# Attention scores of the last two batches as three fp32r products, in a kernel of attention, dense MoE and routed experts

## The chip, the cores and the metric

The kernel runs on one core of one Trainium2 chip. The metric is the device time of one execution in microseconds (us). The core's engines are TensorE (PE, with its weight loads as PEld), VectorE (DVE), ScalarE (ACT), GpSimd (POOL) and SyncE (SP); SP issues nearly all the DMAs.

## The reference

Three stages, each fed by the one before. Inputs are fp32; batch 4, 12 heads, 448 positions, head size 64; the dense stage has 768 columns and 2048 hidden units; the routed stage has 8 experts of 1024.

```python
scores = scale * np.matmul(q, k.transpose(0, 1, 3, 2))
scores = cap * np.tanh(scores / cap)
scores = scores - np.max(scores, axis=-1, keepdims=True)
attn = np.exp(scores)
attn = attn / (np.sum(attn, axis=-1, keepdims=True) + 1e-09)
x = np.matmul(attn, v)
...
h = x @ w_in
g = np.maximum(h, 0.0) ** 2
x = g @ w_out
...
out[mask] = np.maximum(x[mask] @ w1[e], 0.0) @ w2[e]
```

The last line is done for each expert `e`, where `mask` holds the tokens that a greedy routing by the sorted gate logits gives it.

## The kernel before

**Attention** (`attention(b)`, L207) takes a batch in six head pairs `hp`. One tile `qk` (128 x 960) holds a pair: head 0 on partitions 0 to 63, head 1 on 64 to 127; columns 0 to 511 are k in four chunks `c`, the rest is q. `scores(hp, c)` (L225) multiplies in fp32. Chunks 0 to 2 are two matmuls, one for each head on its half of the rows (L234); chunk 3 holds what is left of both heads and is one matmul over all rows (L236). Each fp32 matmul leaves two MATMUL records in the trace. ACT then does tanh (L238) and exp (L239). The sums over the chunks, `z`, are added on POOL from batch 1 on (L245, L247, L251). `pv` (L253) multiplies by v, `norm` (L264) sums z over the partitions on PE (L267), adds an epsilon on ACT (L269), and DVE takes the reciprocal (L270) and multiplies (L272). In the last two batches (`whole`) the pieces of a pair come in larger steps.

**Dense stage.** `hidden(b)` (L387) makes 16 tiles of 18 matmuls of the type fp32r, `output(b)` (L422) six tiles of 48. Every operand is split into a high and a low fp32r part (a cast on ACT, a subtraction on DVE or POOL), and a product is the sum of three, high by high, low by high and high by low (L400 to L402, L457 to L459). The attention's result is split so by `split_rows` (L310). The weights come as 64-bit words: DVE rebuilds fp32 from them in three instructions a tile (L329 to L331), ACT casts the high part (`wh`, L357), POOL or DVE subtracts (`wl`, L358), and both are stored to DRAM (L376), from where the later batches load them. That is done once, beside the first two batches: the 16 tiles of w_in, then the 24 of w_out.

**Order.** `run` (L87) does attention(0), then hidden(0) beside attention(1), then for b = 2 and 3 output(b-2) and hidden(b-1) beside attention(b). `merge` (L906) takes the next piece from the stream that is least far along: each piece yields a number of us, and a stream has a total (118.0 and 44.0). From b = 2 on this written order is PE's own. All the other engines, and SP's DMAs, are put in order by the tile framework's scheduler. Every engine works through its instructions in that order, so an instruction that waits holds up what stands behind it on its engine.

**Names used below.** qk(b, hp) is a pair's tile; it has two buffers (L213), the load is on SP (L219). `load_v` (L221) has three. `g` is the dense stage's hidden tile (cast L411, subtraction L412), `r` its relu and square (L407, L408), `acc` the psum tile it comes from (two buffers), `raw` a tile of 64-bit words (three buffers), `wf` the rebuilt fp32 tile (three). `finish` (L432) transposes an output tile (L435), copies it (L437) into a tile `rows` of two buffers and stores it on ACT's queue (L438). `xt` (pool "rows", seven buffers) holds the tiles before that.

Of the kernel before, what the change touches and what calls it, by code (L numbers as in the profile page):

```python
# [9 lines left out]
F32 = mybir.dt.float32  # L10
F32R = mybir.dt.float32r
# [8 lines left out]
NB, NH, S, DH = 4, 12, 448, 64  # L20
# [3 lines left out]
HP = NH // 2  # L24
KC = 4
KP = S // KC
WAIT = (), (8, 12, 16)
KB = S // 128
# [52 lines left out]
class Kernel:  # L81
# [5 lines left out]
    def run(self):  # L87
        tc = self.tc
        PS = bass.MemoryType.PSUM
        with tc.tile_pool(name="keep", bufs=1) as self.keep, \  # L90
                tc.tile_pool(name="wts", bufs=1) as self.wts, \
                tc.tile_pool(name="psum", bufs=2, space=PS) as self.psum, \
                tc.tile_pool(name="dram", bufs=1, space=bass.MemoryType.DRAM) as self.dram, \
                ExitStack() as right, ExitStack() as left:
            self.setup()
            self.mp = right.enter_context(tc.tile_pool(name="moe1", bufs=1, side="right"))
            self.gpool = self.mp
            xs = right.enter_context(ExitStack())
            self.xp = xs.enter_context(tc.tile_pool(name="x", bufs=ND, side="right"))
            with tc.tile_pool(name="x32", bufs=ND, side="right") as self.xq:  # L100
                with tc.tile_pool(name="rows", bufs=ND + 1, side="right") as self.tp, \
                        tc.tile_pool(name="attn", bufs=2, side="right") as self.ap:
                    merge([(self.attention(0), 44.0)])
                    self.split_rows(0)
                    merge([(self.hidden(0), 58.0), (self.attention(1), 44.0)])
                    for b in range(2, NB):
                        self.split_rows(b - 1)
                        streams = [(chain(self.output(b - 2), self.hidden(b - 1)), 118.0), (self.attention(b), 44.0)]
                        if b == NB - 1:
                            streams.append((self.gate_decode(), 30.0))  # L110
                        with tc.manual_schedule(engines={mybir.EngineType.PE}):
                            merge(streams)
                self.split_rows(NB - 1)
            self.gp = left.enter_context(tc.tile_pool(name="gate", bufs=1))
            last = left.enter_context(ExitStack())
            self.gpool = last.enter_context(tc.tile_pool(name="last", bufs=1))
            with tc.tile_pool(name="gate_load", bufs=3, side="right") as self.gl:
                with tc.manual_schedule(engines={mybir.EngineType.PE}):
                    merge([(self.hidden(NB - 1), 60.0), (self.gate_weights(), 80.0)])
            xs.close()  # L120
            self.tp = right.enter_context(tc.tile_pool(name="rows2", bufs=2, side="right"))
            self.rp = right.enter_context(tc.tile_pool(name="route", bufs=1, side="right"))
            self.router_setup()

            def room():
                last.close()
                self.ep = left.enter_context(tc.tile_pool(name="expert", bufs=2))

            with tc.manual_schedule(engines={mybir.EngineType.PE}):
                self.second(room)  # L130
# [76 lines left out]
    def attention(self, b):  # L207

        nc, ap = self.nc, self.ap
        qk, P, vt, zs, U = {}, {}, {}, {}, {}  # L210
        adder = nc.vector if b == 0 else nc.gpsimd

        def load(hp):  # L213
            qk[hp] = t = ap.tile([128, QK], F32, name="qk", bufs=2)
            if b + hp == 0:
                for half, q in ((0, nc.sync), (1, nc.scalar)):
                    q.dma_start(t[half * 64:half * 64 + 64], self.q_k[b, hp, half * 64:half * 64 + 64])
            else:
                nc.sync.dma_start(t, self.q_k[b, hp])  # L219

        def load_v(hp):  # L221
            vt[hp] = ap.tile([128, KB + 1, 2 * DH], F32, name="v", bufs=3)
            nc.sync.dma_start(vt[hp], self.v[b, hp])

        def scores(hp, c):  # L225

            t = qk[hp]
            n = 2 if c < KB else 1
            k, q = t[:, c * 128:(c + 1) * 128], t[:, QK - S:]
            ps = self.psum.tile([128, 2, 512], F32, name="big")  # L230
            if c < KB:
                for s in range(2):
                    rows = slice(s * 64, s * 64 + 64)
                    nc.tensor.matmul(ps[:, s, :S], k[rows], q[rows], start=True, stop=True)  # L234
            else:
                nc.tensor.matmul(ps[:, 0, :S], k, q, start=True, stop=True)  # L236
            p = ap.tile([128, n, S], F32, name=f"p{n}", bufs=(2, 5)[n - 1])
            nc.scalar.activation(p, ps[:, :n, :S], AF.Tanh, scale=self.isc)  # L238
            e = nc.scalar.activation(p, p, AF.Exp, scale=self.capt)  # L239
            if b == 0:  # L240
                self.exps.append(e)
            P[hp, c] = p
            if c == 1:
                zs[hp] = z = ap.tile([128, 2, S], F32, name="z", bufs=2)
                adder.tensor_add(z, P[hp, 0], p)  # L245
            elif c == 2:
                adder.tensor_add(zs[hp], zs[hp], p)  # L247
            elif c == KB:
                for s in range(2):
                    half = slice(s * 64, s * 64 + 64)  # L250
                    adder.tensor_add(zs[hp][half, s], zs[hp][half, s], p[half, 0])  # L251

        def pv(hp, c0, c1):  # L253
            if c0 == 0:
                U[hp] = self.psum.tile([128, S], F32, name="aux")
            for c in range(c0, c1):
                if c < KB:
                    for s in range(2):
                        nc.tensor.matmul(U[hp][s * 64:s * 64 + 64], vt[hp][:, c, s * 64:s * 64 + 64], P[hp, c][:, s],  # L259
                                         start=(c == 0), stop=False, skip_group_check=True)  # L260
                else:
                    nc.tensor.matmul(U[hp], vt[hp][:, c], P[hp, c][:, 0], start=False, stop=True, skip_group_check=True)

        def norm(hp):  # L264
            z = self.psum.tile([128, S], F32, name="aux")
            for s in range(2):
                nc.tensor.matmul(z[s * 64:s * 64 + 64], self.ones, zs[hp][:, s], start=True, stop=True)  # L267
            d = zs[hp][:, 0]
            (nc.vector.tensor_scalar(d, z, self.eps, None, op0=OP.add) if b == 0 else nc.scalar.activation(d, z, AF.Identity, bias=self.eps))  # L269
            nc.vector.reciprocal(d, d)  # L270
            x = self.xq.tile([128, S], F32, name="x")
            m = nc.vector.tensor_mul(x, U.pop(hp), d)  # L272
            if b == 0:
                self.norms.append(m)
            if b == NB - 1:
                self.mark = m
            self.x_t[b, hp] = x

        load(0)
        load(1)  # L280
        load_v(0)
        whole = b > 1
        for hp in range(HP + 1):
            if hp < HP:
                if hp + 1 < HP:
                    load_v(hp + 1)
                scores(hp, 0)
                if not whole:
                    yield 0.8
                scores(hp, 1)  # L290
                yield 1.6 if whole else 0.8
            if hp:
                pv(hp - 1, 0, 2)
                if not whole:
                    yield 1.6
                pv(hp - 1, 2, 4)
                if not whole or hp == HP:
                    yield 1.6
                norm(hp - 1)
                yield 4.0 if whole else 0.8  # L300
            if hp < HP:
                scores(hp, 2)
                if not whole:
                    yield 0.8
                scores(hp, 3)
                if hp + 2 < HP:
                    load(hp + 2)
                yield 1.4 if whole else 0.6

    def split_rows(self, b):  # L310
        nc = self.nc
# [110 lines left out]
    def output(self, b):  # L422
# [9 lines left out]
        def finish(j, xt):  # L432
            ps = self.psum.tile([KP, KC, 128], F32, name="aux")
            for c in range(KC):
                nc.tensor.transpose(ps[:, c], xt[:, c * KP:(c + 1) * KP], self.c("ident"))  # L435
            o = mp.tile([KP, KC, 128], F32, name="rows", bufs=2)
            (nc.vector.tensor_copy if b == LAST and j == ND - 1 else nc.scalar.copy)(o, ps)  # L437
            nc.scalar.dma_start(  # L438
                rows[j // DA][b, :, :, j % DA * 128:(j % DA + 1) * 128], o)
# [520 lines left out]
```

## Time and profile before

| | |
|---|---|
| runs | 1087.70, 1090.86, 1092.13 us, median 1090.86 |
| profiled execution | 1092.94 us, of which the span is 1091.2 |
| mean granted clock of PE | 0.99 |
| busy PE, DVE, ACT, POOL | 1058.7 (97%), 597.1 (55%), 469.1 (43%), 247.8 (23%) us |
| matmuls of the scores (L234, L236) | 74.7 us and about 2% of the span on the chain that ended last |

The page gives busy time over the whole span. A stage in which a second engine is as full as PE doesn't show there; for that, busy time by stretch is needed. In the timelines a start is in us from the span's start, and a bracket at the end of a row tells how long the engine was idle before it and which instruction ended that. PE's rows overlap, because a matmul's record is longer than the distance to the next one.

### The profile page before, as it was taken

The page shows a single profiled execution, that of the slowest core. Times are in us where ns is not written, and L with a number is a line of the kernel's source. Part 1 is how long each engine was busy: PE and PEld are TensorE (multiplying, and loading weights), DVE is VectorE, ACT ScalarE, POOL GpSimd, SP SyncE. Part 2 cuts the span into 40 slices and gives each one's busy share as a digit, 9 for nine tenths or more (in the row PEclk, how much of TensorE's full clock was granted, in tenths as well). Part 3 has the DMA queues.
Part 4 walks back from the last instruction along what each step waited for, and adds up shares of the span by engine and source line. Part 5 has one row for each costly group of instructions (what it writes and reads, how often), then busy time and mean ns, then how long its engine had stood idle before and what let it go on. Part 6 is the DMA issues. An engine that isn't in the chain of part 4 may idle for free.

```text
span 1091.2 us, 15936 instructions
## 1 busy us (share of the span) xinstructions
PE 1058.7 (97%) x5866; PEld 836.0 (77%) x5866; DVE 597.1 (55%) x1068; ACT 469.1 (43%) x723; POOL 247.8 (23%) x181
## 2 busy tenths in 40 slices
PE   6899999999999999999999999998899999999996
PEld 2336656777678677677888888887799999999996
DVE  5997999997222245465311253445445444676550
ACT  5867686445554533454543000012232222544551
POOL 0217684764221322221000000002220201012000
PEclk9999999999999999999999999998999999999998
DMA  8644777899655499987984467567466257656620
GB/s 280 239 142 149 252 261 259 256 329 322 209 181 174 153 305 331 340 293 267 311 298 134 153 185 249 187 179 225 133 241 233 71 183 246 216 184 218 216 81 26
DMA packets 102494, 237.54 MB, mean 218 GB/s; under 512 B 11088, under 2 KB 21872, under 8 KB 102416
## 3 DMA queue, kind: packets, MB, share of 16 engines
q1 hardware_dynamic: 87776, 219.58, 59.8%
q0 software_dynamic: 3424, 11.19, 3.4%
q10 hardware_dynamic: 11216, 5.75, 2.0%
q8 instruction: 46, 0.75, 0.3%
q14 instruction: 32, 0.26, 0.1%
HBM read 194.01 MB, written 42.47 MB: 217 GB/s over the span
## 4 chain that ended last, share of the span: by engine, by line
PE 76%; issue 11%; DVE 7%; DMA 3%; ACT 2%; POOL 1%; SPq 0%; POOLq 0%; DVEq 0%; ACTq 0%
PE big L885 8%; PE acc L457 8%; PE acc L459 7%; PE acc L458 7%; PE acc L400 7%; PE acc L401 6%; PE acc L402 6%; PE acc L847 5%; PE big L234 4%; PE aux L259 4%; PE aux L661 2%; PE acc L854 2%; PE aux L267 2%; PE big L236 2%; DVE wf L330 1%
## 5 line engine op out<-in xcount | busy, mean ns | idle before, releaser
L457 PE MATMUL acc<-g,wh 128*128 128x448 f32 x384 | 151.5, 394 | 0.0
L400 PE MATMUL acc<-xh,wh 128*128 128x448 f32 x384 | 147.8, 387 | 0.8 <-ACT r L407 0.8
L401 PE MATMUL acc<-xl,wh 128*128 128x448 f32 x384 | 141.0, 367 | 0.8 <-DVE xl L317 0.8
L459 PE MATMUL acc<-g,wl 128*128 128x448 f32 x384 | 140.7, 366 | 0.0
L458 PE MATMUL acc<-g,wh 128*128 128x448 f32 x384 | 140.7, 366 | 0.0
L402 PE MATMUL acc<-xh,wl 128*128 128x448 f32 x384 | 140.1, 365 | 0.0
L885 PE MATMUL big<-wh,g 128*112 128x384 f32 x512 | 118.2, 343 | 0.0
L238 ACT ACTIVATE p<-big,isc 128x896 f32<-128x896 f32 x96 | 85.8, 908 | 44.8 <-PE big L234 36.9
L270 DVE RECIPROCAL z<-z 128x448 f32<-128x448 f32 x24 | 70.7, 2948 | 59.8 <-ACT z L269 59.7
L412 DVE TENSOR_TENSOR g<-r,g 128x448 fp32r<-128x448 f32 x58 | 42.9, 740 | 103.6 <-ACT g L411 103.3
L400 PEld LDWEIGHTS acc<-xh,wh 128*128 128x128 f32 x384 | 71.7, 187 | 33.9 <-issue 14.7
L764 POOL DMA_INDIRECT xg<-x,idx x32 | 34.5, 1078 | 257.0 <-issue 157.7
L239 ACT ACTIVATE p<-p,capt 128x896 f32<-128x896 f32 x96 | 89.4, 948 | 1.5
L885 PEld LDWEIGHTS big<-wh,g 128*112 128x112 f32 x512 | 86.4, 175 | 0.8
L457 PEld LDWEIGHTS acc<-g,wh 128*128 128x128 f32 x384 | 73.0, 190 | 14.4 <-issue 9.6
L401 PEld LDWEIGHTS acc<-xl,wh 128*128 128x128 f32 x384 | 72.4, 189 | 11.4 <-issue 3.4
L234 PE MATMUL big<-qk 64*128 64x448 f32 x288 | 74.7, 602 | 6.5 <-DMA qk<-qk 6.3
L329 DVE TENSOR_SCALAR wf<-raw 128x512 int32<-128x512 int32 (+1 forms) x64 | 52.7, 837 | 46.5 <-DMA raw<-w_out_t 38.1
L407 ACT ACTIVATE r<-acc 128x448 f32<-128x448 f32 x64 | 34.7, 542 | 100.9 <-PE acc L402 87.6
L459 PEld LDWEIGHTS acc<-g,wl 128*128 128x128 f32 x384 | 72.5, 189 | 6.8 <-issue 0.2
L402 PEld LDWEIGHTS acc<-xh,wl 128*128 128x128 f32 x384 | 72.3, 188 | 6.9 <-issue 0.8
L458 PEld LDWEIGHTS acc<-g,wh 128*128 128x128 f32 x384 | 72.9, 190 | 6.0 <-issue 1.7
(181 smaller groups left out, 1865.2 us busy)
## 6 DMA issues: line engine op xcount, KB each, us to landing
g<-w SPq DMA_DIRECT2D x62, 384.0 KB, 6.9
wh<-wih SPq DMA_DIRECT2D x48, 384.0 KB, 3.5
wl<-wil SPq DMA_DIRECT2D x48, 384.0 KB, 5.6
wh<-woh SPq DMA_DIRECT2D x72, 256.0 KB, 3.0
wl<-wol SPq DMA_DIRECT2D x72, 256.0 KB, 2.9
wf<-w SPq DMA_DIRECT2D x33, 384.0 KB, 3.5
raw<-w SPq DMA_DIRECT2D x33, 384.0 KB, 4.4
raw<-w_in SPq DMA_DIRECT2D x16, 768.0 KB, 6.5
```

The costliest lines, as they stand in the source:

```text
L234: nc.tensor.matmul(ps[:, s, :S], k[rows], q[rows], start=True, stop=True)
L238: nc.scalar.activation(p, ps[:, :n, :S], AF.Tanh, scale=self.isc)
L239: e = nc.scalar.activation(p, p, AF.Exp, scale=self.capt)
L270: nc.vector.reciprocal(d, d)
L400: nc.tensor.matmul(ps, wh[:, d], xh, start=(d == 0), stop=False)
L401: nc.tensor.matmul(ps, wh[:, d], xl, start=False, stop=False)
L402: nc.tensor.matmul(ps, wl[:, d], xh, start=False, stop=(d == ND - 1))
L457: nc.tensor.matmul(ps, a, gh, start=(f == 0), stop=False)
L458: nc.tensor.matmul(ps, a, gl, start=False, stop=False)
L459: nc.tensor.matmul(ps, z, gh, start=False, stop=(f == NF - 1))
L847: nc.tensor.matmul(H[j], W[j][0][:, d], xs[:, d, 0].bitcast(F32), start=(d == 0), stop=(d == ND - 1))
L885: nc.tensor.matmul(acc[h][:, s, :DM // 2], l, r[:, s * (DM // 2):(s + 1) * (DM // 2)], start=(j == 0 and first), stop=(j == NF2 - 1 and last))
```

## The change

For batches 2 and 3 a new `split(hp)` makes a high and a low fp32r tile of the pair's `qk`, the cast on ACT and the subtraction on DVE. `scores` then does three fp32r products in place of one fp32 product, on the row halves as before. split(0) comes ahead of the batch's first pair, split(hp+1) behind scores(hp, 3). Each of the two new tiles has one buffer. `load_v(hp+1)` is moved behind norm(hp-1), for all batches; v has two buffers in place of three, `xt` six in place of seven, the output tile `rows` one in place of two. The attention's total is 47 in place of 44, and two of its yields change, which moves its pieces against the dense stage's on PE.

```diff
-                with tc.tile_pool(name="rows", bufs=ND + 1, side="right") as self.tp, \
+                with tc.tile_pool(name="rows", bufs=ND, side="right") as self.tp, \
...
-                        streams = [(chain(self.output(b - 2), self.hidden(b - 1)), 118.0), (self.attention(b), 44.0)]
+                        streams = [(chain(self.output(b - 2), self.hidden(b - 1)), 118.0), (self.attention(b), 47.0)]
...
+        whole = b > 1
...
         def load_v(hp):
-            vt[hp] = ap.tile([128, KB + 1, 2 * DH], F32, name="v", bufs=3)
+            vt[hp] = ap.tile([128, KB + 1, 2 * DH], F32, name="v", bufs=2)
             nc.sync.dma_start(vt[hp], self.v[b, hp])
 
+        def split(hp):
+            h, l = (ap.tile([128, QK], F32R, name=f"qk{i}", bufs=1) for i in "hl")
+            nc.scalar.copy(h, qk[hp])
+            nc.vector.tensor_sub(l, qk[hp], h.bitcast(F32))
+            qk[hp] = (h, h), (h, l), (l, h)
+
         def scores(hp, c):
 
-            t = qk[hp]
             n = 2 if c < KB else 1
-            k, q = t[:, c * 128:(c + 1) * 128], t[:, QK - S:]
+            products = qk[hp] if whole else ((qk[hp], qk[hp]),)
             ps = self.psum.tile([128, 2, 512], F32, name="big")
-            if c < KB:
-                for s in range(2):
-                    rows = slice(s * 64, s * 64 + 64)
-                    nc.tensor.matmul(ps[:, s, :S], k[rows], q[rows], start=True, stop=True)
-            else:
-                nc.tensor.matmul(ps[:, 0, :S], k, q, start=True, stop=True)
+            for i, (x, y) in enumerate(products):
+                k, q = x[:, c * 128:(c + 1) * 128], y[:, QK - S:]
+                first, last = i == 0, i == len(products) - 1
+                if c < KB:
+                    for s in range(2):
+                        rows = slice(s * 64, s * 64 + 64)
+                        nc.tensor.matmul(ps[:, s, :S], k[rows], q[rows], start=first, stop=last)
+                else:
+                    nc.tensor.matmul(ps[:, 0, :S], k, q, start=first, stop=last)
...
-        whole = b > 1
+        if whole:
+            split(0)
+            yield 3.0
         for hp in range(HP + 1):
             if hp < HP:
-                if hp + 1 < HP:
-                    load_v(hp + 1)
                 scores(hp, 0)
...
                 norm(hp - 1)
-                yield 4.0 if whole else 0.8
+            if hp + 1 < HP:
+                load_v(hp + 1)
+            if hp:
+                yield 3.2 if whole else 0.8
             if hp < HP:
                 scores(hp, 2)
...
                 scores(hp, 3)
                 if hp + 2 < HP:
                     load(hp + 2)
-                yield 1.4 if whole else 0.6
+                if whole and hp + 1 < HP:
+                    split(hp + 1)
+                yield 2.2 if whole else 0.6
...
-            o = mp.tile([KP, KC, 128], F32, name="rows", bufs=2)
+            o = mp.tile([KP, KC, 128], F32, name="rows", bufs=1)
```

In the rows of the order that follow, a name's number tells one buffer's use from another, and the bracket lists the engines and DMA queues that an instruction waits for. The line numbers of the changed kernel are 9 to 14 higher from `scores` on.

The first place is ACT's order at the end of attention(1). Here p2_1150 is a score tile of attention(1)'s last pair, acc_1137 a psum tile of hidden(0), and qk_1385 the tile qk(2, 0). Before:

```order
L238 ACTIVATE p1_1118<-big_1116,isc_70 128x448 [waits PE_49]
L408 ACTIVATE r_1110<-r_1110 128x448 [waits Activation_49]
L239 ACTIVATE p1_1118<-p1_1118,capt_66 128x448 [waits Activation_49]
L411 CAST g_1113<-r_1110 128x448 [waits Activation_49]
L238 ACTIVATE p2_1150<-big_1147,isc_70 128x896 [waits PE_49]
L357 CAST wh_1236<-wf_1181 128x512 [waits DMAHW3_49,DVE_49,PE_49]
L407 ACTIVATE r_1170<-acc_1137 128x448 [waits DVE_49,PE_49]
```

After:

```order
L248 ACTIVATE p1_1118<-p1_1118,capt_66 128x448 [waits Activation_49]
L425 CAST g_1113<-r_1110 128x448 [waits Activation_49]
L228 CAST qkh_1391<-qk_1385 128x960 [waits DMAHW5_49]
L247 ACTIVATE p2_1150<-big_1147,isc_70 128x896 [waits PE_49]
L371 CAST wh_1236<-wf_1181 128x512 [waits DMAHW2_49,DVE_49,PE_49]
L421 ACTIVATE r_1170<-acc_1137 128x448 [waits DVE_49,PE_49]
```

The cast of qk(2, 0), which waits for that tile's load, now stands between the cast of g_1113 and the tanh, the cast of wh_1236 and the relu.

The second place is SP's order at the same time: the loads of w_out and of qk, and the stores of the split weights (wih, wil, woh, wol). Before:

```order
L376 DMA wil14_1241<-wl_1130 128x768 [waits DMAHW4_49,Pool_49]
L325 DMA raw_1414<-w_out 128x512 [waits DMAHW5_49,DVE_49]
L219 DMA qk_1385<-qk 128x960 [waits DMAHW6_49,PE_49]
L376 DMA wih15_1298<-wh_1187 128x768 [waits DMAHW7_49,Activation_49]
L376 DMA wil15_1299<-wl_1188 128x768 [waits DMAHW0_49,Pool_49]
L325 DMA raw_1456<-w_out 128x512 [waits DMAHW1_49,DVE_49]
```

After:

```order
L390 DMA wil14_1241<-wl_1130 128x768 [waits DMAHW3_49,Pool_49]
L339 DMA raw_1402<-w_out 128x512 [waits DMAHW4_49,DVE_49]
L220 DMA qk_1385<-qk 128x960 [waits DMAHW5_49,PE_49]
L390 DMA wih15_1298<-wh_1187 128x768 [waits DMAHW6_49,Activation_49]
L390 DMA wil15_1299<-wl_1188 128x768 [waits DMAHW7_49,Pool_49]
L220 DMA qk_1387<-qk 128x960 [waits DMAHW5_49,DMAHW0_49,DVE_49]
L390 DMA woh0_1375<-wh_1236 128x512 [waits DMAHW1_49,Activation_49]
L339 DMA raw_1428<-w_out 128x512 [waits DMAHW2_49,DVE_49]
```

The load of qk(2, 0) stands where it stood, behind a load of w_out that waits for DVE. The next qk tile is now loaded ahead of the w_out tile that used to come, and it waits for DVE (for the subtraction of the first pair, whose tile it overwrites).

The third place is DVE's order between the decode of the twelfth tile of w_out (wf_1656 before, wf_1669 after) and what follows it in attention(2). Before:

```order
L331 SCALAR_TENSOR_TENSOR wf_1627<-raw_1628,wf_1627 128x512 [waits DVE_49]
L329 TENSOR_SCALAR wf_1656<-raw_1657 128x512 [waits DMAHW0_49,DVE_49]
L330 SCALAR_TENSOR_TENSOR wf_1656<-raw_1657,wf_1656 128x512 [waits DVE_49]
L331 SCALAR_TENSOR_TENSOR wf_1656<-raw_1657,wf_1656 128x512 [waits DVE_49]
L270 RECIPROCAL z_1405<-z_1405 128x448 [waits Activation_49]
```

After:

```order
L345 SCALAR_TENSOR_TENSOR wf_1640<-raw_1641,wf_1640 128x512 [waits DVE_49]
L343 TENSOR_SCALAR wf_1669<-raw_1670 128x512 [waits DMAHW0_49,DVE_49]
L344 SCALAR_TENSOR_TENSOR wf_1669<-raw_1670,wf_1669 128x512 [waits DVE_49]
L345 SCALAR_TENSOR_TENSOR wf_1669<-raw_1670,wf_1669 128x512 [waits DVE_49]
L229 TENSOR_TENSOR qkl_1575<-qk_1387,qkh_1574 128x960 [waits PE_49,Activation_49]
L343 TENSOR_SCALAR wf_1712<-raw_1713 128x512 [waits DMAHW1_49,Pool_49]
```

The subtraction for pair 1 of attention(2) stands behind that tile's decode. On PE the pair's first scores, which read qkl_1575, stand about where pv(0) of attention(2) stood before.

## Rows read from the trace of the kernel before

**Rows 1.** Busy time by stretch: us, PE, PEld, DVE, ACT, POOL, clock, DMA, GB/s.

```profile
140.00:170.00 30.00, 30.00 (x129) 18.08 (x126) 29.66 (x19) 22.77 (x35) 26.85 (x15) 1.00 0.73 247
...
200.00:230.00 30.00, 30.00 (x144) 22.07 (x144) 29.54 (x27) 14.37 (x23) 21.26 (x13) 1.00 0.88 288
```

**Rows 2.** PE's timeline around a pair's scores in attention(2): start, us, engine, line.

```profile
301.61 0.37 PE L400 MATMUL acc<-xh,wh 128*128 128x448 f32 x1
...
302.01 0.37 PE L402 MATMUL acc<-xh,wl 128*128 128x448 f32 x1
302.31 1.77 PE L234 MATMUL big<-qk 64*128 64x448 f32 x8
...
304.33 0.36 PE L401 MATMUL acc<-xl,wh 128*128 128x448 f32 x1
```

**Rows 3.** The same timeline, cut at 302.80.

```profile
302.31 1.02 PE L234 MATMUL big<-qk 64*128 64x448 f32 x4
```

**Rows 4.** Timeline of PE's weight loads.

```profile
301.61 0.19 PEld L401 LDWEIGHTS acc<-xl,wh 128*128 128x128 f32 x1
```

**Rows 5.** Groups by form: line, engine, operation, count | busy us, mean ns | idle before.

```profile
L357 ACT CAST wh<-wf 128x768 fp32r<-128x768 f32 x40 | 33.1, 831 | 33.3 <-DMA wf<-w 13.1 <-PE acc L854 9.9 <-PE big L885 6.7
...
L358 DVE TENSOR_TENSOR wl<-g,wh 128x768 fp32r<-128x768 f32 x48 | 45.9, 955 | 22.3 <-ACT wh L357 19.9 <-issue 1.1 <-PE acc L854 0.9
```

**Rows 6.** ACT's timeline at the end of attention(1).

```profile
155.77 0.56 ACT L411 CAST g<-r 128x448 fp32r<-128x448 f32 x1
157.63 1.01 ACT L238 ACTIVATE p<-big,isc 128x896 f32<-128x896 f32 x1 [1.30 <-PE big L234]
...
159.04 0.55 ACT L407 ACTIVATE r<-acc 128x448 f32<-128x448 f32 x1
```

**Rows 7.** SP's timeline: the load of qk(2, 0).

```profile
163.49 0.69 SPq L219 DMA_DIRECT2D qk<-qk  x1
```

**Rows 8.** The loads of L219 in 150 to 180: issue to landing in us.

```profile
DMA to landing us min/median/max: 7.3/7.3/7.3
```

**Rows 9.** PE's timeline: a tile of hidden(0), norm(1, 5), pv(2, 0).

```profile
168.59 0.47 PE L400 MATMUL acc<-xh,wh 128*128 128x448 f32 x1
...
182.90 0.97 PE L267 MATMUL aux<-z,ones 128*64 128x448 f32 x2
...
203.48 1.35 PE L259 MATMUL aux<-p,v 128*64 128x448 f32 x6
```

**Rows 10.** DVE's timeline.

```profile
161.38 1.65 DVE L331 SCALAR_TENSOR_TENSOR wf<-raw,wf 128x512 int32<-128x512 int32 x1
...
166.54 0.61 DVE L412 TENSOR_TENSOR g<-r,g 128x448 fp32r<-128x448 f32 x1
167.07 2.33 DVE L329 TENSOR_SCALAR wf<-raw 128x512 int32<-128x512 int32 x1
...
171.75 0.42 DVE L329 TENSOR_SCALAR wf<-raw 128x512 int32<-128x512 int32 x1
...
178.18 0.61 DVE L272 TENSOR_TENSOR x<-aux,z 128x448 f32<-128x448 f32 x1
...
212.57 0.69 DVE L331 SCALAR_TENSOR_TENSOR wf<-raw,wf 128x512 int32<-128x512 int32 x1
```

**Rows 11.** POOL's timeline: what runs beside the third of those rows.

```profile
166.76 2.35 POOL L245 TENSOR_TENSOR z<-p,p 128x896 f32<-128x896 f32 x1 [2.72 <-DVE x L272]
```

**Rows 12.** ACT's timeline: two copies of output tiles in a row.

```profile
255.26 0.57 ACT L437 COPY rows<-aux 112x512 f32<-112x512 f32 x1
...
266.78 0.59 ACT L437 COPY rows<-aux 112x512 f32<-112x512 f32 x1 [2.45 <-PE aux L435]
```

**Rows 13.** Issue to landing of those stores.

```profile
DMA to landing us min/median/max: 3.3/4.8/8.4
```

**Rows 14.** PE's timeline in attention(0): an idle stretch.

```profile
20.47 1.66 PE L267 MATMUL aux<-z,ones 128*64 128x448 f32 x3 [3.10 <-DVE z L251]
```

**Rows 15.** Busy time by stretch, behind it; columns as in Rows 1.

```profile
20.60:24.00 3.40, 3.40 (x8) 0.85 (x7) 2.51 (x4) 0.00 (x0) 0.00 (x0) 0.51 0.88 293
```

## The prediction

> **What bounds the kernel now.** I first read the busy time by stretch, because a mean over the span hides where a second engine is full. In 140 to 170 and in 200 to 230 PE is busy for the whole 30 us, at a granted clock of 1.00, and so is DVE, for 29.66 and 29.54 us [rows 1]. That is the stage in which the weights are rebuilt on DVE. The reader is to see two things: there a us more or less on PE is a us of the whole, and work that is put on DVE there has no free place. Next come PE's timeline, for the price of a score, and the timelines of ACT, SP and DVE at the places of the order shown above, for what the new instructions wait for.
>
> **PE: the gain.** A normal fp32r matmul starts every 0.20 us (two steps from 301.61 to 302.01) [rows 2]. Chunks 0 and 1 of a pair stand between the L402 at 302.01 and the L401 at 304.33; less the 0.20 of that L402 and of the L400 between them, they hold PE for 1.92 us. Their four fp32 products are eight records, two passes each [rows 2]. By 302.80 four of these have begun [rows 3]; one after the other at 0.20 us, the fourth would begin only at 302.91. So the two heads' halves run side by side, in four slots of about 0.37 us (four fill the 1.77 with a tail), and the remaining 0.4 us is the change to half rows and back. Chunks 2 and 3 are again four slots of two passes (one product on halves, one on all rows), so I count a pair as 2 x 1.92 = 3.84 us. After, chunks 0 and 1 are six slots of halves, chunks 2 and 3 three and three: twelve slots of 0.203, with the same 0.4 twice 3.27 us. The gain is 0.57 us a pair, 6.8 us for twelve pairs. Since PE is full there, all of it counts, if PE is not made to wait.
>
> The slots' price rests on fp32r loads of weights staying hidden: the load for L401 starts at 301.61 with the L400 of the same rows [rows 4], and the matmuls keep their 0.20.
>
> **ACT and DVE: the added work.** The cast of 128 x 960 is 960/768 of one of 0.831 us, 1.04 us; the subtraction is 960/768 of 0.955, 1.19 us [rows 5]; twelve of each. As busy time on ACT this is free, PE doesn't wait for ACT's throughput. On DVE, in the full stretch, it is not. Beside POOL a DVE row can be several times as long: the same L329 takes 2.33 us while POOL adds z from 166.76 on [rows 11], and 0.42 at 171.75 [rows 10]. So 1.19 is the lower end, some 2.5 the upper.
>
> **First wait: ACT behind a load.** The cast of qk(2, 0) stands in ACT's order ahead of the tanh of p2_1150. Before, ACT was through with the g cast at 156.33, the tanh began at 157.63 and the relu at 159.04 [rows 6]. But qk(2, 0) left SP only at 163.49 [rows 7], behind a load of w_out that waits for the decode which ends at 163.03 [rows 10], and took 7.3 us to land [rows 8], till about 170.5 counted from the issue's start, perhaps a us sooner. The order on SP is the same after. So ACT stands from 156.3 to about 170. Then come the cast 1.0 and what was 157.63 to 159.59 from tanh to the relu's end, 2.0: the relu is done at 172.6. The hidden(0) tile at 168.59 [rows 9] needs the psum buffer that this relu frees, so PE waits 4.0 us (bounds 2, if the load comes earlier, and 5). DVE's subtraction of g, 166.54 [rows 10], waits for ACT's cast of the same g, behind exp, square and cast (2 us more), till 174.6: 8 us in which DVE, which has no slack, stands still.
>
> Directly behind this is norm(1, 5) at 182.90 [rows 9]: its psum buffer is free when DVE has done the multiplication of 178.18 [rows 10]. With DVE 8 us behind and PE 6, 0 to 5 us are lost; I take 1, since most of the 8 is covered by PE's own lag and the 4 us between the two.
>
> **Second wait: qkl of pair 1 on DVE.** In DVE's new order this subtraction comes behind the twelfth decode of w_out, before done at 212.57 + 0.69 = 213.3 [rows 10]. PE comes to the pair's first scores about where pv(2, 0) was, 203.48 [rows 9]; with the first wait, its clock (below) and the 1 us, 210.2. The subtraction ends at 213.3 + 1.2 (that of pair 0) + 1.2 = 215.7 if DVE has made up its 8 us, because POOL too has less to do meanwhile, and at 223.7 if it hasn't: PE waits 5.5 or 13.5 us. A DVE which runs in its short forms throughout could take all of it away, so the lower bound is 0. I take 8, near the lower of the two, because the long forms leave DVE room to catch up. This wait doesn't depend on the first: without it DVE is 8 us earlier, but so is PE by 6.7. Pairs 2 and 3 stand behind further decodes: 0 to 3 us, I take 1. From 264 on no decode of these weights is left, and in attention(3) the cast and the subtraction have room.
>
> **The clock.** After 3.10 us without work [rows 14] PE ran 3.40 us at 0.51, its 1.2 GHz level [rows 15], which costs 1.7 us. Two long waits: 3.4 us; bounds 0 and 3.4.
>
> **Edits at nothing.** The output tile with one buffer: copies are at least 11.5 us apart [rows 12], a store lands 8.4 us after its issue at most [rows 13]; without this cover the transposes would wait for up to some 3 us each. v with two buffers, loaded behind the norm: a 256 KB load in the place of another, needed a whole pair later. The xt tiles: six are written a batch, and read long before the next batch's.
>
> **The sum.** -6.8 + 4.0 + 1.7 + 1 + 8 + 1.7 + 1 = +10.6 us, on the profiled execution's 1092.9 a time of 1103.5. The median is 2.1 below that execution, so 1101.5, **1102 us**. With the bounds (waits of 2, 0, 5.5, 0 and one drop of the clock, or 5, 5, 13.5, 3 and two) this case reaches from 1093 to 1114.
>
> **The rivals.** What a measurement of this kernel can tell from no change is about 0.5%, 5.5 us: 1085.4 and 1096.3.
>
> *DVE catches up, ACT's wait stays.* The qkl of pair 1 is ready at 210. For it: half of DVE's rows there are long forms. Against: 29.54 of 30 us busy [rows 1], and two subtractions more. -6.8 + 4.0 + 1.7 + 1 is 0: 1091.
>
> *Faster: both waits are covered.* The place is ACT's cast of qk(2, 0): if its load lands by 157.6 no wait starts, and DVE loses no time. The load would have to leave SP some 13 us sooner than at 163.49, or the scheduler's place for the cast be harmless; and qkl of pair 1 would have to be done by 203.5, 10 us ahead of its decode's end before. Then the gain of 6.8 stands alone: 1084. It decides when all waits and clock drops are together under 1.3 us.
>
> *The halves don't run side by side in fp32r.* Nine slots of a pair are doubled, 9 x 0.203 x 12 = 22 us: 1124. Against: fp32 halves do [rows 3], and nothing in the edit changes the rows they use.
>
> *Weight loads come into the open.* In the twelve slots of a pair two or three products follow each other on the same rows. If a load had to wait for the matmul ahead of it, each slot would be 0.19 us longer [rows 4], 144 x 0.19 = 27 us: 1129. Against: the normal matmuls alternate weights on the same rows at 0.20. The Trainium skill ("TensorE: Matmul & The Clock Gate", Part 3, "The mechanism") has a rule by which this would come: a weight load overlaps a running matmul only if its row group differs. The load at 301.61 [rows 4] speaks against that sentence, the same section's mention of a background weight buffer for it.
>
> **How the numbers follow.** Forecast 0.61, DVE catches up 0.17, both covered 0.14, halves in series 0.05, loads in the open 0.03. The range, 1084 to 1114, takes in the first three cases and leaves out the last two and the edges, under 0.2. Slower by over 0.5%: the forecast less its lower edge, and the last two, 0.65; within 0.5%: the second case and that edge, 0.21; faster: 0.14. The forecast's own range is 1093 to 1114.
>
> **What would show it.** On ACT an idle stretch of over 10 us ahead of a cast of qkh, released by the load; then PE's L400 released by ACT's relu, about 4 us. In 200 to 225 PE's first L243 of pair 1 with 5 to 13 us idle, released by DVE's qkl. PEclk near 0.5 behind each. Chunks 0 and 1 at 1.6 us in place of 1.92. If PE shows no idle stretch over 2 us before 270, the forecast is wrong; if the scores take more than 1.92, the gain is.

## The result, and the profile after

The changed kernel takes 1102.61 us (median of 6 runs, 1098.42 to 1111.18), the kernel before in the same comparison 1089.92. The ratio is 1.0124, with an interval from 1.0088 to 1.016: slower by some 13 us, where 1102 was forecast. The profiled execution has a span of 1102.8 us, against 1091.2.

The waits of PE come first. The view lists for each line of PE what it waited for: us in total, times, longest.

```profile
PE big L243 <- DVE qkl L229: 9.5, 1, 9.5
...
PE acc L414 <- ACT r L421: 2.9, 3, 2.2
...
PE big L245 <- ACT p L247: 0.9, 1, 0.9
```

None of these three stood in the list of before in this size; 0.8 of the second did. They are the two forecast waits and a small third. ACT's timeline at the end of attention(1), which answers to [rows 6], shows how the second comes about:

```profile
156.29 0.56 ACT L425 CAST g<-r 128x448 fp32r<-128x448 f32 x1
168.50 0.99 ACT L228 CAST qkh<-qk 128x960 fp32r<-128x960 f32 x1 [11.65 <-DMA qk<-qk]
169.40 1.00 ACT L247 ACTIVATE p<-big,isc 128x896 f32<-128x896 f32 x1
...
170.81 0.55 ACT L421 ACTIVATE r<-acc 128x448 f32<-128x448 f32 x1
```

The cast stands 11.65 us for its tile, and the tanh, which PE had made ready long before, stands behind it. The load left SP as late as before, [rows 7], and landed sooner than there, [rows 8]; first its row of SP's timeline, then the times to landing of the loads of L220 in 150 to 172:

```profile
163.03 0.38 SPq L220 DMA_DIRECT2D qk<-qk  x1
```

```profile
DMA to landing us min/median/max: 4.2/4.8/5.5
```

163.03 and 5.5 give 168.5, the start of the cast. The relu's end at 171.36 lets PE go on, at half speed; PE's timeline:

```profile
171.40 0.74 PE L414 MATMUL acc<-xh,wh 128*128 128x448 f32 x1 [2.22 <-ACT r L421]
171.94 0.57 PE L415 MATMUL acc<-xl,wh 128*128 128x448 f32 x1
```

The second place is pair 1 of attention(2). DVE's timeline, to compare with the last of [rows 10], and then PE's:

```profile
216.07 1.63 DVE L345 SCALAR_TENSOR_TENSOR wf<-raw,wf 128x512 int32<-128x512 int32 x1
217.63 2.08 DVE L229 TENSOR_TENSOR qkl<-qk,qkh 128x960 fp32r<-128x960 f32 x1
```

```profile
209.75 0.47 PE L243 MATMUL big<-qkh 64*128 64x448 f32 x2
219.76 0.74 PE L243 MATMUL big<-qkl,qkh 64*128 64x448 f32 x2 [9.54 <-DVE qkl L229]
```

PE does the first product, which needs only the high part, at 209.75 and then waits for the low part. ACT had the high part cast by 209.52; DVE comes to the subtraction 8 us later, behind the twelfth decode, the row ahead of it. DVE is full up to there. Behind it, it isn't: in the rest of the stretch up to 264 it is idle for 11 of 44.3 us, 9.0 of them until POOL's subtractions of the weights end (busy time by stretch, columns as in [rows 1]):

```profile
200.00:219.70 19.70, 9.28 (x49) 7.47 (x47) 19.56 (x21) 11.75 (x17) 13.51 (x8) 0.81 0.86 273
219.70:264.00 44.30, 44.24 (x213) 33.27 (x213) 33.20 (x35) 21.42 (x30) 21.50 (x14) 0.93 0.80 264
```

The small third wait, for a tanh at chunk 3 of pair 0, is DVE's too, by way of ACT: that tanh stands four instructions behind a cast, ahead of which ACT was idle until DVE's multiplication of a norm ended.

```profile
200.84 0.57 ACT L330 CAST xh<-x 128x448 fp32r<-128x448 f32 x1 [7.38 <-DVE x L281]
```

The clock after both waits, by stretch (columns as in [rows 1]):

```profile
171.40:174.80 3.40, 3.40 (x9) 2.81 (x9) 3.33 (x4) 3.33 (x5) 2.39 (x2) 0.54 0.94 228
...
219.70:223.00 3.30, 3.24 (x13) 2.47 (x14) 3.27 (x6) 2.05 (x3) 1.00 (x1) 0.50 0.83 210
223.00:227.00 4.00, 4.00 (x16) 3.60 (x15) 0.94 (x2) 2.72 (x5) 1.89 (x1) 0.66 1.01 396
```

The first wait costs 3.40 x 0.46 = 1.6 us of clock, the second 3.24 x 0.50 + 4.00 x 0.34 = 3.0.

The gain is there as well. PE's timeline around chunks 0 and 1 of a pair, which answers to [rows 2]:

```profile
196.28 0.37 PE L473 MATMUL acc<-g,wl 128*128 128x448 f32 x1
196.58 0.47 PE L243 MATMUL big<-qkh 64*128 64x448 f32 x2
196.89 0.36 PE L243 MATMUL big<-qkl,qkh 64*128 64x448 f32 x2
197.09 0.37 PE L243 MATMUL big<-qkh,qkl 64*128 64x448 f32 x2
...
198.31 0.37 PE L472 MATMUL acc<-g,wh 128*128 128x448 f32 x1
```

The two halves of a product are one row of x2, rows follow at 0.20 us, and from L473 to L472 it is 2.03 us, less two normal slots of 0.203 so 1.62, against 1.92 before. Twelve pairs at twice 0.29 are 6.9 us. (The 74.7 us of the scores in the table of before are L234 alone; L236 has another 23.9.)

A longer stretch shows the same. The dense stage's high-by-low product (L402 before, L416 after) runs 96 times a batch, and between its 192nd and its 288th all of attention(3) runs beside it. The view of a line counts its matmuls and gives the first and the last start, here two rows of before and two of after:

```profile
L402 PE MATMUL acc<-xh,wl x192: 360/363/709, 33.3 to 354.8; 128*128 128x448 f32 x192
L402 PE MATMUL acc<-xh,wl x288: 360/363/709, 33.3 to 525.6; 128*128 128x448 f32 x144
...
L416 PE MATMUL acc<-xh,wl x192: 360/363/709, 33.7 to 368.4; 128*128 128x448 f32 x192
L416 PE MATMUL acc<-xh,wl x288: 360/363/709, 33.7 to 535.7; 128*128 128x448 f32 x144
```

170.8 us before, 167.3 after: 3.5 us for six pairs, 0.58 a pair. At the 288th the change is 10.1 us behind; the other 1.5 of the 11.6 between the two spans arise later, where there are no scores any more.

### The profile page after: what moved, and what is told of

Same layout as the page of the kernel before. It is cut to its first block, busy times and chain, and to the rows that moved or that the text cites. A ratio compares the mean times of both kernels' runs of the same rounds, so it can differ in the third digit from the quotient of the medians.

```text
span 1102.8 us, 16139 instructions
## 1 busy us (share of the span) xinstructions
PE 1056.0 (96%) x5950; PEld 848.4 (77%) x5950; DVE 605.9 (55%) x1080; ACT 478.3 (43%) x735; POOL 246.3 (22%) x181
## 4 chain that ended last, share of the span: by engine, by line
PE 68%; issue 12%; DVE 12%; DMA 4%; ACT 2%; POOL 1%; SPq 0%; POOLq 0%; DVEq 0%; ACTq 0%
PE big L899 8%; PE acc L471 7%; PE acc L473 7%; PE acc L472 6%; PE acc L414 6%; PE acc L415 5%; PE acc L416 5%; PE acc L861 5%; PE aux L268 3%; PE big L243 3%; DVE wf L344 3%; PE aux L675 2%; PE acc L868 2%; DVE wf L343 2%; PE aux L276 1%
## 5 line engine op out<-in xcount | busy, mean ns | idle before, releaser
L472 PE MATMUL acc<-g,wh 128*128 128x448 f32 x384 | 141.4, 368 | 0.0
L473 PE MATMUL acc<-g,wl 128*128 128x448 f32 x384 | 141.2, 368 | 0.0
L416 PE MATMUL acc<-xh,wl 128*128 128x448 f32 x384 | 140.6, 366 | 0.0
L416 PEld LDWEIGHTS acc<-xh,wl 128*128 128x128 f32 x384 | 72.7, 189 | 6.9 <-issue 0.8
L473 PEld LDWEIGHTS acc<-g,wl 128*128 128x128 f32 x384 | 72.9, 190 | 6.4 <-issue 0.2
L472 PEld LDWEIGHTS acc<-g,wh 128*128 128x128 f32 x384 | 73.3, 191 | 5.6 <-issue 0.9
L372 POOL TENSOR_TENSOR wl<-wf,wh 128x512 fp32r<-128x512 f32 (+1 forms) x33 | 55.5, 1686 | 86.9 <-ACT wh L371 76.9
L256 POOL TENSOR_TENSOR z<-z,p 128x896 f32<-128x896 f32 x18 | 40.2, 2233 | 147.2 <-ACT p L248 146.0
```

Of the source, the lines that this page charges most:

```text
L372: low.tensor_sub(wl[:, :w], wf[:, :w], wh[:, :w].bitcast(F32))
L416: nc.tensor.matmul(ps, wl[:, d], xh, start=False, stop=(d == ND - 1))
L472: nc.tensor.matmul(ps, a, gl, start=False, stop=False)
L473: nc.tensor.matmul(ps, z, gh, start=False, stop=(f == NF - 1))
```

## The experiments

All times are medians, all ratios against runs of the kernel before on the same chip in the same comparison.

**The new order and the pools, without split.** The two calls of `split` are taken out, `products` is one fp32 product.

```diff
-            products = qk[hp] if whole else ((qk[hp], qk[hp]),)
+            products = ((qk[hp], qk[hp]),)
...
```

> The changed kernel without split: scores are again one fp32 product, everything else (PE's order, the yields, v, xt and output tiles) as changed. My theory (the loss is two waits that the split brings, on ACT's cast of pair 0 and on DVE's subtraction of pair 1, the gain of some 6.8 us is real): with neither, within 3 us of before, 1087 to 1093. Rival A (the new order and the smaller pools cost the time): as slow as the change or slower by the lost gain, 1100 to 1110.

1095.39 against 1091.27 us, ratio 1.0034 (1.0013 to 1.0054): 3.7 us slower. That is neither. Rival A as the main cause falls, but the new order isn't free, as I had taken it to be. PE waits in a place of its own (waits of PE, 100 to 560):

```profile
PE aux L276 <- ACT rows L448: 1.9, 1, 1.9
```

A norm waits for a psum buffer that ACT's copy of an output tile has still to free.

**Only the added work.** The tiles are split, the scores read fp32 `qk`.

```diff
             nc.vector.tensor_sub(l, qk[hp], h.bitcast(F32))
-            qk[hp] = (h, h), (h, l), (l, h)
...
```

> Cast and subtraction are done as in the change, but the scores read qk in fp32, so nothing waits for the split tiles. My theory: ACT still stands some 11 us at the first cast, PE waits 2 us for the relu and loses 1.5 us of clock; no wait on qkl, no gain: 1091 to 1096. Rival B (the added work itself, on a DVE that is full, costs the time): the 12.7 us of the change and the 6.8 us that are not gained, 1103 to 1110.

1118.09 us, ratio 1.0252 (1.0225 to 1.0279): slower than the change itself, and outside of both expectations. Little of it is DVE's, as rival B would have it. From 100 to 560 PE waits for 19.4 us, all of it for ACT, in the main here:

```profile
PE aux L275 <- ACT rows L450: 8.2, 2, 5.1
PE aux L448 <- ACT z L277: 4.9, 1, 4.9
```

Only 3.2 of the 19.4 us, for two tanh, go back to DVE, by the way of the third wait above. ACT's own waits in 150 to 300 show the cause of most others:

```profile
ACT qkh L228 <- DMA qk<-qk: 40.9, 5, 11.7
```

In the change, a cast of a later pair also waits until PE has read the buffer it writes, and so stands late in ACT's order, when its load has long landed. With nothing on PE reading that buffer the scheduler puts the casts early, and ACT stands for a load five times: 11.7 us for the first, and again 9.9 and 10.65:

```profile
220.94 0.99 ACT L228 CAST qkh<-qk 128x960 fp32r<-128x960 f32 x1 [9.90 <-DMA qk<-qk]
...
250.52 0.99 ACT L228 CAST qkh<-qk 128x960 fp32r<-128x960 f32 x1 [10.65 <-DMA qk<-qk]
```

It is the first wait's mechanism, repeated. What I had overlooked is that taking PE's reads away moves the casts.

**Split only in the last batch**, in the new order: `split` and the three products where `b == NB - 1`.

> Split and three products only in the last batch, where no weight is rebuilt beside it; fp32 scores in batch 2. My theory: half the gain, 3.4 us, and neither wait: 1085 to 1089. Rivals A and B: no better than before, 1090 or more. If fp32r on the row halves gained nothing: 1090.

1091.98 us, ratio 1.001 (0.9994 to 1.0027). Not faster than before, but 2.6 us better by ratio than the same order without any split, though the two intervals overlap. The trace has the gain: from the 192nd to the 288th product 167.3 us, against 170.8 without split. So the last batch gains, and the order takes it away again; the wait on the copy is there too, 1.9 us.

**The late cast.** The cast of pair 0 goes behind the last exp of the attention before.

```diff
-            nc.scalar.copy(h, qk[hp])
+            with self.tc.issue_after(self.last_exp.ins) if hp == 0 else nullcontext():
+                nc.scalar.copy(h, qk[hp])
...
```

> Only the cast of pair 0 is put behind the last exp of the attention before, on ACT. My theory: ACT's stretch of 11 us is gone and with it PE's first wait (2.2 and 1.5 of clock); but the subtraction of pair 1 still stands behind the twelfth decode, and DVE gains only the 2.5 us that it stood idle, so that PE, earlier by 3.7, waits longer there: 11 in place of 9.5. Total 0 to 3 us better than the change: 1099 to 1103. If the two waits simply add up: 1098 to 1099. If only the first wait counts: 1088 to 1092.

1099.71 us, ratio 1.0079 (1.0054 to 1.0104), against 1.0124 for the change. By the ratios it is 4.9 us better, by the medians 2.9; the intervals overlap. In the profile the first wait is gone, and the second is as long as it was:

```profile
214.91 0.74 PE L244 MATMUL big<-qkl,qkh 64*128 64x448 f32 x2 [9.54 <-DVE qkl L230]
```

I had expected PE to wait longer there, since it comes earlier. But DVE comes earlier by as much (its subtraction starts at 212.77, not 217.63), as the prediction had it: the two waits add up.

**The early subtraction.** The eleventh and later decodes of w_out are put behind pair 1's subtraction on DVE.

```diff
-            with self.after(self.norms, WAIT[0], n):
+            with self.tc.issue_after(self.low.ins) if self.low and n >= 26 else nullcontext():
...
```

> Only DVE's order is touched: the eleventh and later decodes of w_out are put behind the subtraction of pair 1, which so stands behind the tenth decode in place of the twelfth. ACT's early cast stays. My theory (the 9.5 us are the two decodes ahead of the subtraction in DVE's order): PE waits there only for cast and subtraction, 1 to 4 us, and loses less clock; 7 to 11 us better than the change, 1092 to 1096. Rival (DVE is full, so the wait only moves): PE waits for the next weights of w_out instead, 1099 to 1103.

1101.71 us, ratio 1.0106 (1.0074 to 1.0137): no better that can be told. PE's timeline says why, at pair 1 and then at pair 2:

```profile
211.60 0.47 PE L245 MATMUL big<-qkl,qkh 64*128 64x448 f32 x2 [1.26 <-DVE qkl L229]
```

```profile
245.17 0.74 PE L245 MATMUL big<-qkl,qkh 64*128 64x448 f32 x2 [8.18 <-DVE qkl L229]
```

At pair 1 the wait falls to 1.26, as my theory had it, and 8.18 us come up at pair 2, behind the decodes that were put off. The rival was right that the wait moves, though not to the weights of w_out.

**Both mended.**

> The late cast of pair 0 and the early subtraction of pair 1 together. My theory: both waits gone but for 1 to 4 us: late_cast's 1099.7 less 7 to 11, so 1089 to 1093; what is left above the gain of 6.9 is the new order and the one-buffer output tile (order_only lost 3.7). Rival (the wait only moves to the weights of w_out): 1096 to 1100.

1098.2 us, ratio 1.0082 (1.0053 to 1.0111), the same as the late cast alone, with the same 8.16 us at pair 2. So the place in DVE's order decides only which pair waits. The cause of this wait is DVE, which has next to no free time up to the subtraction that is waited for: here it is busy for 39.54 of the 40.3 us from 200 to 240.3, in the change for 19.56 of the 19.7 to 219.7.

**The output tile with two buffers again**, in the order without split.

```diff
-            o = mp.tile([KP, KC, 128], F32, name="rows", bufs=1)
+            o = mp.tile([KP, KC, 128], F32, name="rows", bufs=2)
```

> order_only with two buffers for the output tile, as before. There PE waited 1.9 us at a norm for ACT's copy of an output tile, which I put down to the store of the tile before it in the same buffer. If so: the 1.9 us and with them up to 1 us more go, 1091 to 1094. If it is the new order alone that makes the norm meet the copy: 1095, the wait unchanged.

1098.13 us, ratio 1.0065 (1.0044 to 1.0086), slower than both expectations; the wait on the copy is still there, 3.0 us:

```profile
PE aux L276 <- ACT rows L448: 3.0, 1, 3.0
```

The one buffer isn't its cause. Behind this wait PE ran at the lower clock; behind the 1.9 us with one buffer it hadn't. By stretch, two rows of this run and one of that:

```profile
242.20:246.00 3.80, 3.71 (x9) 2.17 (x10) 3.77 (x5) 2.04 (x3) 2.83 (x2) 0.50 1.04 359
246.00:250.00 4.00, 4.00 (x15) 3.64 (x14) 3.90 (x5) 1.05 (x2) 1.89 (x2) 0.68 1.05 266
...
240.00:250.00 10.00, 8.37 (x41) 7.12 (x42) 9.86 (x10) 5.26 (x9) 6.70 (x4) 1.00 0.89 304
```

That is 3.71 x 0.50 + 4.00 x 0.32 = 3.1 us, most of the 3.4 by which this version is slower than the other by ratio.

**The old order with the late cast.** Total and yields as before the change (44, 4.0, 1.4), no step for split(0).

> The change with the late cast and with the old total and yields (44, 4.0, 1.4, no step for split(0)), so that PE's pieces stand as before the change. In DVE's order the subtraction of pair 1 now stands behind the eighth decode of w_out (done at about 197 before), and PE wants it at 197. My theory: PE waits 2 to 5 us there, the cost of the new order is not paid, gain 6.9: 1084 to 1091. Rival (pairs so close that every pair's cast and subtraction is waited for, some 1 us each): 1093 to 1098.

1097.88 us, ratio 1.008 (1.0056 to 1.0104), in the range of the rival. PE waits for the split tiles at pairs 0, 1 and 2; for pair 1's cast 1.67 us, and at pair 2:

```profile
233.60 0.47 PE L244 MATMUL big<-qkl,qkh 64*128 64x448 f32 x2 [4.36 <-DVE qkl L230]
```

The same wait again, in smaller pieces: it isn't the new order that makes it.

**The subtractions on POOL**, for the first four pairs of batch 2, with the late cast.

```diff
-            nc.vector.tensor_sub(l, qk[hp], h.bitcast(F32))
+            (nc.gpsimd if b == 2 and hp < 4 else nc.vector).tensor_sub(l, qk[hp], h.bitcast(F32))
```

> The late cast, and the subtractions of the first four pairs of batch 2 on POOL in place of DVE. Theory as the runs so far leave it (DVE is full until its decodes end, so a subtraction there is either waited for or pushes the next one late): with DVE freed, PE waits at pairs 1 to 3 only for the chain of psum, ACT's cast and POOL's subtraction, under 4 us each, no wait of 8 us anywhere: 1092 to 1098. If POOL's queue is as late as DVE's: a wait of over 7 us on qkl again, 1098 or more.

1100.66 us, ratio 1.0094 (1.0066 to 1.0121). The long wait is gone, but the time isn't better. In its place there are six of 0.6 to 2.1 us in the same stretch, among them

```profile
225.34 0.65 PE L450 MATMUL aux<-cf,xt 128*112 128x128 f32 x4 [2.14 <-ACT z L279]
...
267.91 0.47 PE L244 MATMUL big<-qkl,qkh 64*128 64x448 f32 x2 [1.82 <-POOL qkl L230]
```

which add up to about 8 us. That this would give the time back was wrong. It leaves DVE as full as it was before the change: busy for 151.79 of 154 us from 110 to 264, against 151.54.

```profile
110.00:264.00 154.00, 147.27 (x664) 101.49 (x663) 151.79 (x122) 91.42 (x138) 103.43 (x57) 0.98 0.79 263
```

So the long wait was for the subtraction on DVE, but no run shows a place in this stage where the added work costs nothing. Why ACT is late at some of these places stays open.

**The pools alone**: fp32 scores, the old total and yields.

> fp32 scores, the old total and yields, so PE's order of before; only the smaller pools of v, xt and the output tile and the later load of v are left of the change. If the new order costs what order_only lost: as before, 1089 to 1092, no wait of PE on ACT's copy of an output tile. If the pools cost it: 1094 or more.

1092.41 us, ratio 1.0015 (0.9997 to 1.0032): no difference that can be told, no wait of PE on the copy. With this, what the version without split lost is put down to the new order, not the pools. By the times alone the two intervals overlap; the absent wait, and the table at the end of this section, tell them apart.

**Split only in the last batch, old order.**

> Split and three products only in the last batch, with the old total and yields. Theory: six pairs' gain of 0.58 us, no wait, no cost of a new order: 3.4 us under before, 1086 to 1089. If split costs the last batch as much as it gains: 1090 to 1092.

1087.5 us, ratio 0.9981 (0.9964 to 0.9997): faster than both kernels, if by little; 2 us by ratio, 2.65 by the medians, where 3.4 were expected. From 100 to 560 PE waits nowhere but 0.8 us for a relu, as before. DVE is as full as ever in 200 to 230, and nothing of split is asked of it there:

```profile
200.00:230.00 30.00, 30.00 (x144) 21.88 (x144) 29.55 (x27) 15.19 (x23) 20.89 (x13) 1.00 0.89 290
```

**Pairs 4 and 5 of batch 2 as well.** I put these two behind the end of the decodes.

> As last_old, and pairs 4 and 5 of batch 2 split too: their scores come after 264, when DVE's decodes are done. Theory: eight pairs' gain, 4.6 us under before, 1085 to 1088, faster than the kernel before and the change. If pair 4 still meets the decodes: a wait on qkl of over 1 us and no better than last_old.

1094.57 us, ratio 1.0038 (1.0022 to 1.0054): a miss. There is no wait on qkl. But the cast of pair 4 is now the first of its buffer, nothing holds it back, and it stands on ACT ahead of its load. Behind it come two tanh, an exp and the copy of an output tile (ACT's timeline), and a norm on PE waits for that copy (PE's):

```profile
258.62 0.99 ACT L228 CAST qkh<-qk 128x960 fp32r<-128x960 f32 x1 [6.40 <-DMA qk<-qk]
...
262.39 0.57 ACT L450 COPY rows<-aux 112x512 f32<-112x512 f32 x1
```

```profile
263.11 1.76 PE L276 MATMUL aux<-z,ones 128*64 128x448 f32 x4 [4.20 <-ACT rows L450]
```

It is the change's first wait in another place.

**All versions at one point.** The start of the 288th high-by-low product, in us from the span's start, lies behind all scores:

| version | 288th starts | against before |
|---|---|---|
| last batch only, old order | 521.8 | -3.8 |
| last batch only, new order | 523.8 | -1.8 |
| the pools alone | 524.7 | -0.9 |
| before | 525.6 | |
| pairs 4 and 5 as well | 527.6 | +2.0 |
| new order and pools, no split | 527.7 | +2.1 |
| both mended | 530.1 | +4.5 |
| late cast | 530.2 | +4.6 |
| the same order with two output buffers, no split | 531.3 | +5.7 |
| subtractions on POOL | 531.8 | +6.2 |
| old order, late cast | 531.9 | +6.3 |
| early subtraction | 534.8 | +9.2 |
| the change | 535.7 | +10.1 |
| only the added work | 548.9 | +23.3 |

It is one profiled execution of each, and the first of these products starts at 32.3 to 34.9 us, so a difference of 1 or 2 us says little. Over that the table tells more than the medians do, since what lies behind this point took between 561 and 568 us, without an order that follows the edits. From the 192nd to the 288th product all five versions with fp32 scores take 170.8 to 170.9 us, the one with only the added work among them, and all nine with split in the last batch 167.3: there the gain comes whole, and the cast and the subtraction cost 0.1 us at most. All other differences of the table arise ahead of the 192nd.

## Why the prediction was right, step by step

The forecast, 1102 us, its direction and its two places came true. By its own steps:

- **The gain on PE**, 6.8 us: 0.58 us a pair is measured, around chunks 0 and 1 and over attention(3), 6.9 in all. The halves run side by side in fp32r. The rivals of halves in series and of weight loads in the open are out: rows of x2 at 0.20 us leave no room for either. The sentence of the Trainium skill ("TensorE: Matmul & The Clock Gate", Part 3, "The mechanism") by which a weight load overlaps a running matmul only where the row groups differ doesn't hold in this form here: three products in a row use the same rows at 0.20 us.
- **The first wait**, 4.0 us: 2.2 measured. The mechanism is as told, and shown by taking it away (the late cast) and by the two versions in which the cast came early again. The size was off because I took 7.3 us for the load from a row of before; here it took 5.5 at most, and PE came to its tile 0.6 us later. What I had follow from it on DVE was wrong: DVE was to stand still for 8 us, since its next subtraction of g would wait for a late cast. But the cast that it needs was done ahead of ACT's stand, at 156.85. DVE didn't wait there; it stood 2.49 us for the split tile:

```profile
166.08 0.61 DVE L426 TENSOR_TENSOR g<-r,g 128x448 fp32r<-128x448 f32 x1
...
169.52 1.16 DVE L229 TENSOR_TENSOR qkl<-qk,qkh 128x960 fp32r<-128x960 f32 x1 [2.49 <-ACT qkh L228]
```

- **norm(1, 5)**, 1 us: nothing.
- **The second wait**, 8 us: 9.5 measured. The subtraction ended at 219.7, where I had put 215.7 to 223.7; PE came at 209.75, where I had 210.2. The 8 was a choice between two cases, DVE level with before and DVE 8 us late, and neither came: its twelfth decode ended at 217.70, 4.4 us later than before (pair 0's subtraction among them), and the subtraction took 2.08 us in place of 1.2. That 8 is so near to 9.5 is in part luck. The step that the runs correct is the cause: I named the twelfth decode ahead of the subtraction. Moved ahead of it, the wait came up at the next pair. It is the DVE that is full up to there, of which the place in the order is only the form. That the wait doesn't depend on the first was right. The rival that DVE would catch up was not borne out.
- **Pairs 2 and 3**, 1 us: no wait on qkl there; 0.95 us for a tanh at chunk 3 of pair 0, which I hadn't seen.
- **The clock**, 3.4 us: 1.6 and 3.0, so 4.6.
- **Edits at nothing**: the pools are (the version with them alone), the new order isn't. I gave it no price; without the split it cost 3.7 us by ratio, 2.1 at the 288th product. The change's own terms sum to -6.9 + 2.2 + 1.6 + 9.5 + 0.95 + 3.0 = 10.4 us. At the 288th product the change is 10.1 us behind; the 1.5 by which its span is longer still arise behind all scores, in a stretch that scatters by 7 us between executions.

So the total was closer than its terms, by luck: the first wait and norm(1, 5) were 2.8 us too dear, the second wait and the clock 2.7 too cheap, and the gain exact. Nor do the two waits, gone, give the time back: with the late cast and POOL's subtractions neither is left, and smaller ones take their place. What is shown is that the loss arises in batch 2, beside the decodes, and how it does in the change.

What beats both kernels is the part of the change that lies behind the decodes: split in the last batch alone, in the old order.

## What to carry to other kernels

Before work is given to an engine to save time on another, look at that engine's busy time in the stretch where the work would fall, not over the span: DVE was 55% busy in all and over 98% where this change needed it, and moving the work in DVE's order only moved the wait. An instruction that waits for a load should not stand ahead of instructions that another engine waits for; the scheduler put it there in four of these versions, where nothing else held it back, and at the first of these places ACT stood for 6 to 12 us, so look at the order for the first use of every new buffer. And test a part of such a change in the stage that has room for it: half of the gain without any of the waits was worth more than all of it with them.

## What the runs showed of the hardware

- A wait of PE can cost more than its length. After 2.22 us without work PE ran at its 1.2 GHz level for about 3 us (0.54 over 3.40), after 9.54 us for about 6 (0.50 over 3.24, 0.66 over the next 4.00): 1.6 and 3.0 us on top. After the 1.95 us for the copy in the new order without split the granted clock stayed at 1.00.
- fp32r products on 64 rows go side by side on the two halves, a pair of them in the 0.20 us of one matmul on all rows; a pair of fp32 halves of the same size took 0.37 us for each of two passes.
- The subtraction of 128 x 960 on DVE took 1.16 us or 2.08 (169.52 and 217.63 in the changed kernel); on POOL it took 2.44 to 2.59.
